# Attention and two MLPs in one kernel: where P is divided, and which operand of P x V is stationary

## The chip, the cores and the metric

The kernel runs on one core of a Trainium2 chip. Time is the device time of one execution in microseconds, and lower is better. The kernel before takes 892.09 us (median of three runs, 891.72 to 892.2). The profile comes from one further execution, of 890.85 us.

## The reference

There are 4 batches, 8 heads, 576 positions and a head size of 64, all in fp32. Heads 0 to 3 see the last 32 positions, heads 4 to 7 see every earlier position of the same residue modulo 32. Two MLPs with squared ReLU follow.

```python
scores = scale * np.matmul(q, k.transpose(0, 1, 3, 2))
mask_local = (rel >= 0) & (rel < stride)                      # heads 0-3
mask_strided = (rel >= 0) & (pos[None, :] % stride == pos[:, None] % stride)   # heads 4-7
scores = np.where(masks[None], scores, -1e9)
attn = np.exp(scores - np.max(scores, axis=-1, keepdims=True))
attn = attn / (np.sum(attn, axis=-1, keepdims=True) + 1e-09)
x = np.matmul(attn, v)                       # -> (2304, 512)
for w_in, w_out in (moe, moe2):              # (512, 2048), (2048, 512)
    x = np.square(np.maximum(x @ w_in, 0)) @ w_out
```

## The kernel before

**The MLPs.** They are what TensorE does most of the time. A layer works on 5 blocks of tokens (512, and one of 256); a block has 16 steps, one for each 128 columns of the hidden width. Products are exact to fp32 by splitting both operands in a high and a low part of type fp32r and adding three products. A step `s` of the main loop issues `mm1(s + 1)`, 12 products of 128x512 into `ps_h`, and then `mm2(s)`, 12 products into `ps_y`. At the end of `mm1`, ScalarE takes the ReLU (`r`, L744) and the square (`gh`, L752), and VectorE the square in fp32 and its low part (`sq`, L753; `gl`, L754). All products have the line L696.

**The attention.** It is cut in 48 fills, numbered 0 to 47, 12 for each batch: a fill is two heads and one piece of the positions. A local fill has 2 groups of 96 queries with 128 keys for each head; a strided one has two groups of 126, two of 108 or one of 108 queries, with as many keys. Of a batch's 12 fills, 6 are local, and of each strided kind there are 2. The MLP of layer 1 needs X of a block before that block starts, so batch 1 runs alone at the start, and batches 2, 3 and 4 run between the products of the blocks 0, 1 and 2 of layer 1.

**The stages of a fill in batches 3 and 4** (fills 24 to 47) are these, and the functions that hold them:
- `split_qk` (L324): q and k are split in high and low parts, two instructions on ScalarE (`qs` L332, `k` L333) and two on VectorE (L334, L337), and the next q and k are loaded into the one buffer for them.
- `scores_first`, `scores_second` (L351): the scores of either head, fp32r.
- `mask_first`, `mask_second` (L379, L381): mask, scale and the negative row maximum, on VectorE.
- `exponent` (L484): one instruction on ScalarE for each head and group.
- `turn_p` (L491): P is transposed by TensorE, one instruction for each head and group; `keep_p` (L499) copies it to SBUF on ScalarE.
- `values` (L507): for each head and group one plain fp32 matmul. Its stationary operand is transposed P (96, 108 or 126 columns), its moving operand is V with a column of ones (65 columns), so that the row sums come with X. It then loads the V of a later fill.
- `divide` (L538 to L541): on VectorE, the sums plus 1e-9, their reciprocal, and X times it.
- `turn_x` (L553): X of both heads is transposed, one instruction for each group.
- `keep_x` (L592) copies X to the MLP's operand as its high part on ScalarE, `rest_x` (L596) subtracts it from X for the low part on VectorE. A fill that lies over a border of blocks does it in parts.

**The order.** A round is one pass through the list `BETWEEN` (L625), in which `(fn, back)` means that the stage `fn` is done for the fill that is `back` fills behind the round's own. So different fills are in different stages at a time. The list has ten places. The rounds of all batches stand one behind the other in `att`, and `att_to` (L650) works them off up to a place. It is called at points in the MLP: `mm1` has a point after each of its first three groups of three products, one stands after `mm1`, three lie in `mm2`, and one follows it, eight to a step. `spans` (L1021) and `point` (L1054) spread the places of a batch evenly over 116 points of its block; in blocks 1 and 2 of layer 1 these are 150 and 120 places. A place whose list is empty only takes room in this spread.

**Queues.** Each engine works its instructions in order. All loads and stores go by the queue of SP, in program order. All PSUM tiles of these fills come in turn from three banks of the pool `ps_a`; `ps_h` has one bank. The tiles `s`, `pt`, `m` and `den` have two buffers each, and V has five.

Of the kernel before, what the change touches and what calls it, by code (L numbers as in the profile page):

```python
# [9 lines left out]
F32 = mybir.dt.float32  # L10
F32R = mybir.dt.float32r
I32 = mybir.dt.int32
AF = mybir.ActivationFunctionType
ALU = mybir.AluOpType
AX = mybir.AxisListType

P = 128
B, H, S, D = 4, 8, 576, 64
STRIDE = 32
NPOS = S // STRIDE  # L20
# [6 lines left out]
BLOCKS = [  # L27
    [(0, TB), (TB, TB), (2 * TB, TB), (3 * TB, TB // 2), (NT - TB, TB)],
    [(0, TB // 2)] + [(n * TB + TB // 2, TB) for n in range(4)],
]  # L30
# [21 lines left out]
FIRST_2 = 2  # L52


SFILLS = [(0, 7, 2), (14, 6, 2), (26, 6, 1)]
LQ, LK = 2 * QB, 2 * QB + STRIDE
# [28 lines left out]
def pack_local(q, k, v):  # L85


    qk = np.zeros((B, 2, 3, P, 2 * LQ + LK), np.float32)
    ov = np.ones((B, 2, 3, P, 2, 2, D + 1), np.float32)
    kp = np.zeros((B, 4, STRIDE + S, D), np.float32)  # L90
    vp = np.zeros((B, 4, STRIDE + S, D), np.float32)
    kp[:, :, STRIDE:] = k[:, :4]
    vp[:, :, STRIDE:] = v[:, :4]
    for u in range(2):
        for f in range(3):
            for h in range(2):
                n, rows = 2 * u + h, slice(h * D, (h + 1) * D)
                qk[:, u, f, rows, h * LQ:(h + 1) * LQ] = q[:, n, f * LQ:(f + 1) * LQ].transpose(0, 2, 1)
                qk[:, u, f, rows, 2 * LQ:] = kp[:, n, f * LQ:f * LQ + LK].transpose(0, 2, 1)
                for g in range(2):  # L100
                    k0 = f * LQ + g * QB
                    ov[:, u, f, :, h, g, :D] = vp[:, n, k0:k0 + P]
    return qk, ov.reshape(B, 2, 3, P, VW)


def pack_strided(q, k, v, fill):

    r0, n, ng = fill
    m = n * NPOS
    w = ng * m  # L110
    qk = np.zeros((B, 2, P, 3 * w), np.float32)
    ov = np.ones((B, 2, P, 2, ng, D + 1), np.float32)

    def rows_of(x):
        x = x[:, 4:].reshape(B, 4, NPOS, STRIDE, D)[:, :, :, r0:r0 + n * ng]
        return x.transpose(0, 1, 3, 2, 4).reshape(B, 4, w, D)

    qq, kk, vv = rows_of(q), rows_of(k), rows_of(v)
    for u in range(2):
        for h in range(2):  # L120
            rows = slice(h * D, (h + 1) * D)
            qk[:, u, rows, h * w:(h + 1) * w] = qq[:, 2 * u + h].transpose(0, 2, 1)
            qk[:, u, rows, 2 * w:] = kk[:, 2 * u + h].transpose(0, 2, 1)
            for g in range(ng):
                ov[:, u, :m, h, g, :D] = vv[:, 2 * u + h, g * m:(g + 1) * m]
    return qk, ov.reshape(B, 2, P, 2 * ng * (D + 1))


def both_halves(qk, w, groups):


    rest = qk.shape[-1] - 2 * w
    kw = rest if groups is None else (groups - 1) * (w // groups) + P
    t = np.zeros(qk.shape[:-1] + (2 * w + 2 * kw,), np.float32)
    for h in range(2):
        rows = slice(h * D, (h + 1) * D)
        for half in (slice(0, D), slice(D, P)):
            t[..., half, h * w:(h + 1) * w] = qk[..., rows, h * w:(h + 1) * w]
            k0 = 2 * w + h * kw
            t[..., half, k0:k0 + rest] = qk[..., rows, 2 * w:]  # L140
    return t


def r32(ap):
    return ap.bitcast(F32)
# [3 lines left out]
def tile_attention_then_two_mlps(  # L149
# [9 lines left out]
    nc = tc.nc  # L159
# [6 lines left out]
    apool = ctx.enter_context(tc.tile_pool(name="att", bufs=2))  # L166
# [128 lines left out]
    fills = []  # L295
# [7 lines left out]
    SPLIT = FIRST_2 * PER_B  # L303
    kin, vin = {}, {}
    n_in, n_vin = [0], [0]

    def src_of(i):
        b, u, kind, f = fills[i]
        arrays, at = (loc, (u, f)) if kind == "l" else (st[f], (u,))
        qk0, qk, v = arrays  # L310
        return (qk0[(b,) + at] if b < FIRST_2 else qk[(b - FIRST_2,) + at]), v[(b,) + at]

    def load_qk():
        i = n_in[0]
        if i >= NFILL:
            return
        n_in[0] += 1
        qk = src_of(i)[0]
        tag = "qk" + str(i % 3 if i < SPLIT else 0)
        kin[i] = fpool.tile([P, QK_COLS[tag]], F32, tag=tag, name="qk", bufs=1)  # L320
        nc.sync.dma_start(out=kin[i][:, :qk.shape[-1]], in_=qk)
# [76 lines left out]
    def load_v():  # L398
        i = n_vin[0]
        if i >= NFILL:  # L400
            return
        n_vin[0] += 1
        _, v = src_of(i)
        vin[i] = vfpool.tile([P, VW], F32, tag="v", name="v", bufs=5)
        nc.sync.dma_start(out=vin[i][:, :v.shape[-1]], in_=v)
# [6 lines left out]
    def x_at(n):  # L412

        return 0 if n == TB else 48

    def x_tiles(j):
        if j not in xh:
            xh[j], xl[j] = (x_tile(t, j % 3) for t in ("xh", "xl"))
        return xh[j], xl[j]

    def geometry(i):

        b, u, kind, f = fills[i]
        if kind == "l":
            return QB, P, 2, QB
        r0, n, ng = SFILLS[f]
        m = n * NPOS
        return m, m, ng, m

    def ps_tile(i, name):  # L430

        n_ps[0] += 1
        if fills[i][0] == 0 and n_ps[0] % 7 < KC:
            return ps_y.tile([P, 512], F32, tag=f"y{n_ps[0] % 7}", name=name)
        return ps_a.tile([P, 512], F32, tag="a", name=name)

    n_ps = [0]
    s_ps, s_sb, mx, pt_ps, pt_sb, o_ps, xn, x_ps = ({} for _ in range(8))
    W = D + 1

# [38 lines left out]
    def exponent(i):  # L479
        nq, nk, ng, _ = geometry(i)  # L480
        s, m = s_sb[i], mx.pop(i)
        for j in range(2 * ng):
            blk = s[:nq, j * nk:(j + 1) * nk]
            nc.scalar.activation(out=blk, in_=blk, func=AF.Exp, scale=-1.0, bias=m[:nq, j:j + 1])  # L484

    def turn_p(i):
        nq, nk, ng, _ = geometry(i)
        s = s_sb.pop(i)
        ps = pt_ps[i] = ps_tile(i, "ps_pt")
        for j in range(2 * ng):  # L490
            nc.tensor.transpose(  # L491
                ps[:nk, j * nq:(j + 1) * nq], s[:nq, j * nk:(j + 1) * nk], ident[:nq, :nq]
            )
# [65 lines left out]
    def x_parts(i):  # L559

        b, u, kind, f = fills[i]
        ps = x_ps[i]
        parts = []
        if kind == "l":
            c = u
            t0, t1 = b * S + f * LQ, b * S + (f + 1) * LQ
            for j, (b0, nb) in enumerate(BLOCKS[0]):
                lo, hi = max(t0, b0), min(t1, b0 + nb)
                if lo < hi:
                    parts.append((j, ps[:, lo - t0:hi - t0], lambda x, a=lo - b0, e=hi - b0, o=x_at(nb): x[:, c, o + a:o + e]))  # L570
        else:
            c = 2 + u
            r0, n, ng = SFILLS[f]
            n *= ng
            src = ps[:, :n * NPOS].rearrange("p (r i) -> p i r", i=NPOS)
            i0 = b * NPOS
            for j, (b0, nb) in enumerate(BLOCKS[0]):
                o, nt = x_at(nb), nb
                b0, nb = b0 // STRIDE, nb // STRIDE
                lo, hi = max(i0, b0), min(i0 + NPOS, b0 + nb)  # L580
                if lo < hi:
                    parts.append((
                        j,
                        src[:, lo - i0:hi - i0],
                        lambda x, a=lo - b0, e=hi - b0, o=o, nt=nt: x[:, c, o:o + nt].rearrange(
                            "p (i r) -> p i r", r=STRIDE)[:, a:e, r0:r0 + n],
                    ))
        return parts

    def keep_x(i):  # L590
        for j, src, place in x_parts(i):
            nc.scalar.activation(out=place(x_tiles(j)[0]), in_=src, func=AF.Copy)  # L592

    def rest_x(i):
        for j, src, place in x_parts(i):
            nc.vector.tensor_tensor(  # L596
                out=place(xl[j]), in0=src, in1=place(r32(xh[j])), op=ALU.subtract
            )
        x_ps.pop(i)
# [23 lines left out]
        [],  # L623
    ]
    BETWEEN = [  # L625
        [(scores_first, 0), (mask_first, 0)],
        [(turn_p, 1)],
        [(keep_p, 1)],
        [(scores_second, 0), (mask_second, 0)],
        [(split_qk, -1)],  # L630
        [(turn_x, 2)],
        [(keep_x, 2)],
        [(rest_x, 2), (exponent, 0)],
        [(values, 1), (divide, 1)],
        [],
    ]
    att = []
# [375 lines left out]
    for k, s in first.items():  # L1013

        s, lag, each = (first[NB], 2, 1) if k == NB + 1 else (s - 12, 3, 2)
# [7 lines left out]
    with tc.manual_schedule():  # L1023
# [3 lines left out]
        ps = ps_h.tile([P, TB], F32, tag="h", name="ps_w")[:, :P]  # L1027
# [18 lines left out]
        for s in range(len(steps)):  # L1046
            k, f = steps[s]
            layer, j = blocks[k]
# [68 lines left out]
```

## Time and profile before

| | before |
|---|---|
| median of three runs | 892.09 us |
| the profiled execution | 890.85 us, span 889.1 us |
| TensorE busy | 870.4 us (98%) |
| VectorE busy | 630.7 us (71%) |
| ScalarE busy | 491.1 us (55%) |
| values, P x V (L507), all batches | 352 instructions |
| transposes of X (L553), all batches | 88 instructions |

A busy time is the union of an engine's instructions. TensorE's instructions are pipelined: a row of one lasts longer than the engine is taken by it, and neighbours overlap. In the timeline, equal neighbours are merged in a row with their count; its first number is the start from the beginning of the span, its second the duration from the first start to the last end. Plain fp32 matmuls count twice, since each is two instructions; transposes and fp32r products count once.

### The profile page before, as it was taken

Reading aid. Unit: us, or ns where it says so; the run is one execution under the profiler, and the core shown is the slowest. Engines: PE = TensorE matmul, PEld = TensorE weight load, DVE = VectorE, ACT = ScalarE, POOL = GpSimd, SP = SyncE. Lnnn points to the kernel's source line nnn. Section 1 sums busy time; section 2 is a strip of 40 time slices with the busy share of each in tenths; the row PEclk is TensorE's granted clock in tenths of the full one; section 3 lists DMA queues with packets and bytes.
Section 4 is the critical chain, followed back from the end, with each engine's and each line's share of the span. In section 5 each row is a group of like instructions: output and inputs, shape, how many; then the busy total and the mean of one; then the engine's idle time right before and its main releaser. Section 6 shows DMA issues by size and latency. Waiting matters only on the chain.

```text
span 889.1 us, 14160 instructions
## 1 busy us (share of the span) xinstructions
PE 870.4 (98%) x5290; PEld 762.1 (86%) x5290; DVE 630.7 (71%) x1521; ACT 491.1 (55%) x987; POOL 0.2 (0%) x4
## 2 busy tenths in 40 slices
PE   9699999999999999999999999999999999999997
PEld 8578878888888888899888898899999999999996
DVE  6999973477765666322299996677787787778676
ACT  6787863455555554232377885545545555555443
POOL 0000000000000000000000000000000000000000
PEclk9799999999999999999999999999999999999999
DMA  8966610222223210010566530100020010001001
GB/s 264 322 216 222 197 42 19 83 79 71 71 77 98 80 52 24 2 48 1 175 209 208 166 131 13 48 13 13 1 73 18 8 49 24 24 1 49 1 1 48
DMA packets 45940, 72.02 MB, mean 81 GB/s; under 512 B 3504, under 2 KB 32304, under 8 KB 45872
## 3 DMA queue, kind: packets, MB, share of 16 engines
q1 hardware_dynamic: 45872, 71.12, 24.5%
q8 instruction: 42, 0.69, 0.3%
q14 instruction: 26, 0.21, 0.1%
HBM read 61.67 MB, written 9.44 MB: 80 GB/s over the span
## 4 chain that ended last, share of the span: by engine, by line
PE 87%; DVE 9%; ACT 2%; issue 1%; ACTq 0%; DVEq 0%
PE ps_h L696 41%; PE ps_y L696 21%; PE ps_y L917 17%; PE ps_o L507 3%; DVE raw L223 2%; PE ps_pt L491 2%; DVE w L268 1%; DVE val L234 1%; PE ps_s L351 1%; PE ps_s L448 1%; DVE raw L220 1%; DVE gl L754 1%; PE ps_x L553 1%; DVE s L468 1%; DVE xl L596 1%
## 5 line engine op out<-in xcount | busy, mean ns | idle before, releaser
L696 PE MATMUL ps_h<-xh,w 128*128 128x512 f32 (+1 forms) x1344 | 401.0, 364 | 0.0
L696 PEld LDWEIGHTS ps_h<-xh,w 128*128 128x128 f32 x1344 | 245.0, 188 | 39.0
L696 PE MATMUL ps_h<-xl,w 128*128 128x512 f32 (+1 forms) x640 | 235.9, 369 | 0.0
L696 PE MATMUL ps_y<-gh,w 128*128 128x512 f32 (+1 forms) x640 | 157.2, 375 | 0.0
L696 PEld LDWEIGHTS ps_h<-xl,w 128*128 128x128 f32 x640 | 120.9, 189 | 14.8 <-DVE xl L596 0.2
L696 PEld LDWEIGHTS ps_y<-gh,w 128*128 128x128 f32 x640 | 107.7, 188 | 16.4 <-ACT gh L750 0.2
L744 ACT ACTIVATE r<-ps_h 128x512 f32<-128x512 f32 x80 | 47.7, 596 | 120.5 <-PE ps_h L696 83.8
L753 DVE TENSOR_TENSOR sq<-r 128x512 f32<-128x512 f32 x50 | 34.6, 692 | 101.6 <-ACT r L744 101.4
L861 DVE TENSOR_TENSOR xl<-wf,xh 128x768 fp32r<-128x768 f32 (+1 forms) x80 | 80.0, 1010 | 15.6 <-ACT xh L860 15.3
L696 PE MATMUL ps_y<-gl,w 128*128 128x512 f32 (+1 forms) x324 | 85.4, 371 | 0.0
L738 DVE TENSOR_TENSOR sq<-sq 128x512 f32<-128x512 f32 x64 | 44.1, 689 | 53.1 <-ACT sq L737 53.1
L860 ACT ACTIVATE xh<-wf 128x768 fp32r<-128x768 f32 (+1 forms) x80 | 68.9, 880 | 22.0 <-PE ps_y L917 22.0
L737 ACT ACTIVATE sq<-ps_h 128x512 f32<-128x512 f32 x64 | 37.8, 591 | 71.8 <-PE ps_h L696 64.9
L917 PE MATMUL ps_y<-xh,gbl 128*128 128x256 f32 x256 | 70.9, 277 | 0.3 <-DVE gbl L861 0.3
L917 PE MATMUL ps_y<-xh,gbh 128*128 128x256 f32 x256 | 71.1, 278 | 0.0
L917 PE MATMUL ps_y<-xl,gbh 128*128 128x256 f32 x256 | 70.9, 277 | 0.0
L754 DVE TENSOR_TENSOR gl<-sq,gh 128x512 fp32r<-128x512 f32 x80 | 55.2, 691 | 20.6 <-ACT gh L750 14.6
L696 PEld LDWEIGHTS ps_y<-gl,w 128*128 128x128 f32 x324 | 55.3, 188 | 8.8
L484 ACT ACTIVATE s<-s,m 96x128 f32<-96x128 f32 (+2 forms) x176 | 55.6, 388 | 5.2 <-DVE m L468 4.8
L917 PE MATMUL ps_y<-xl,gah 128*128 128x256 f32 x192 | 53.3, 278 | 0.2 <-DVE xl L861 0.2
L917 PE MATMUL ps_y<-xh,gal 128*128 128x256 f32 x192 | 53.2, 277 | 0.2 <-DVE gal L882 0.2
L917 PE MATMUL ps_y<-xh,gah 128*128 128x256 f32 x192 | 53.3, 278 | 0.0
(77 smaller groups left out, 1347.0 us busy)
## 6 DMA issues: line engine op xcount, KB each, us to landing
raw<-moe_w_in_d SPq DMA_DIRECT2D x32, 512.0 KB, 4.7
raw<-moe_w_out_d SPq DMA_DIRECT2D x32, 512.0 KB, 4.0
qk<-loc_qk_d SPq DMA_DIRECT2D x12, 416.0 KB, 3.2
out_d<-o SPq DMA_DIRECT2D x18, 256.0 KB, 2.3
y_dram<-o SPq DMA_DIRECT2D x16, 256.0 KB, 2.1
y_in<-y_dram SPq DMA_DIRECT2D x16, 256.0 KB, 3.0
qk<-loc_qk_d SPq DMA_DIRECT2D x12, 304.0 KB, 4.0
v<-loc_v_d SPq DMA_DIRECT2D x24, 130.0 KB, 2.5
```

What stands on the lines that cost most here:

```text
L223: nc.vector.scalar_tensor_tensor(out=lower, in0=upper, scalar=-(2 ** 31), in1=lower, op0=ALU.bitwise_and, op1=ALU.bitwise_or)
L484: nc.scalar.activation(out=blk, in_=blk, func=AF.Exp, scale=-1.0, bias=m[:nq, j:j + 1])
L507: nc.tensor.matmul(ps[:nq, j * W:(j + 1) * W], lhsT=pt[:nk, j * nq:(j + 1) * nq], rhs=t[:nk, j * W:(j + 1) * W], start=True, stop=True,)
L696: nc.tensor.matmul(y[:, c:c + w], lhsT=lhsT, rhs=rhs[:, c:c + w], start=start and c == 0, stop=stop and c + w == n,)
L737: nc.scalar.activation(out=t, in_=ps, func=AF.Relu, scale=W_BACK)
L738: nc.vector.tensor_tensor(out=t, in0=t, in1=t, op=ALU.mult)
L744: nc.scalar.activation(out=r, in_=ps, func=AF.Relu, scale=W_BACK)
L753: nc.vector.tensor_tensor(out=sq, in0=r, in1=r, op=ALU.mult)
L754: nc.vector.tensor_tensor(out=lo, in0=sq, in1=r32(h), op=ALU.subtract)
L860: nc.scalar.activation(out=hi, in_=src, func=AF.Copy)
L861: nc.vector.tensor_tensor(out=lo, in0=src, in1=r32(hi), op=ALU.subtract)
L917: nc.tensor.matmul(y[:, t * HALF:(t + 1) * HALF], lhsT=a[:, i, rows], rhs=w[:, cols], start=first and t == 0 and m == 0, stop=end and t == ...
```

## The change

It touches the fills of batches 3 and 4 alone. The exponents also give the row sums (`exponent_and_sums`), `divide_p` divides P by them in place on VectorE, ahead of the transposing. `values_of_both` then does one matmul for each group: its stationary operand is V of both heads side by side (128 columns, packed so on the host, without the column of ones), its moving operand transposed P of both heads. The result is X already transposed, with head 0 in the partitions 0 to 63 of the first half of its columns and head 1 in the partitions 64 to 127 of the second half; the other quarters aren't read. `turn_x` and `divide` drop out. `keep_x` and `rest_x` take X by halves of 64 partitions (`x_parts_of_both`), and where a local fill lies over a border of blocks, also by group. The places of the stages in a round are new; the values of a fill come one round after its scores, as before, and its X in that same round rather than in the one behind.

```diff
+def heads_together(v, groups):
+    v = v.reshape(v.shape[:-1] + (2, groups, D + 1))[..., :D]
+    return np.ascontiguousarray(v.swapaxes(-3, -2)).reshape(v.shape[:-3] + (groups * P,))
...
+    def exponent_and_sums(i):
+        nq, nk, ng, _ = geometry(i)
+        s, m = s_sb[i], mx.pop(i)
+        d = dens[i] = apool.tile([P, 4], F32, tag="den", name="den")
+        for j in range(2 * ng):
+            blk = s[:nq, j * nk:(j + 1) * nk]
+            nc.scalar.activation(
+                out=blk, in_=blk, func=AF.Exp, scale=-1.0, bias=m[:nq, j:j + 1],
+                accum_out=d[:nq, j:j + 1],
+            )
+
+    def divide_p(i):
+        nq, nk, ng, _ = geometry(i)
+        d = dens.pop(i)[:nq, :2 * ng]
+        nc.vector.tensor_scalar_add(out=d, in0=d, scalar1=1e-9)
+        nc.vector.reciprocal(out=d, in_=d)
+        s = s_sb[i][:nq, :2 * ng * nk].rearrange("q (j k) -> q j k", j=2 * ng)
+        nc.vector.tensor_tensor(
+            out=s, in0=s, in1=d.unsqueeze(2).to_broadcast([nq, 2 * ng, nk]), op=ALU.mult
+        )
+
+    def values_of_both(i):
+        nq, nk, ng, _ = geometry(i)
+        pt = pt_sb.pop(i)[:nk, :2 * ng * nq].rearrange("k (h g q) -> k h g q", h=2, g=ng)
+        v = vin.pop(i)
+        ps = x_ps[i] = ps_tile(i, "ps_x")
+        for g in range(ng):
+            nc.tensor.matmul(
+                ps[:, 2 * g * nq:2 * (g + 1) * nq],
+                lhsT=v[:nk, g * P:(g + 1) * P],
+                rhs=pt[:, :, g],
+                start=True,
+                stop=True,
+            )
+        load_v()
+
+    def x_parts_of_both(i):
+        b, u, kind, f = fills[i]
+        nq, nk, ng, _ = geometry(i)
+        parts = []
+        for h in range(2):
+            rows = slice(h * D, (h + 1) * D)
+            ps = x_ps[i][rows, :2 * ng * nq].rearrange("p (g h q) -> p h g q", g=ng, h=2)[:, h]
...
     def keep_x(i):
-        for j, src, place in x_parts(i):
+        for j, src, place in (x_parts if i < SPLIT else x_parts_of_both)(i):
             nc.scalar.activation(out=place(x_tiles(j)[0]), in_=src, func=AF.Copy)
 
     def rest_x(i):
-        for j, src, place in x_parts(i):
+        for j, src, place in (x_parts if i < SPLIT else x_parts_of_both)(i):
...
     BETWEEN = [
-        [(scores_first, 0), (mask_first, 0)],
+        [(divide_p, 1), (scores_first, 0), (mask_first, 0)],
+        [],
+        [(scores_second, 0), (mask_second, 0)],
         [(turn_p, 1)],
         [(keep_p, 1)],
-        [(scores_second, 0), (mask_second, 0)],
         [(split_qk, -1)],
-        [(turn_x, 2)],
-        [(keep_x, 2)],
-        [(rest_x, 2), (exponent, 0)],
-        [(values, 1), (divide, 1)],
+        [(values_of_both, 1)],
+        [(keep_x, 1), (exponent_and_sums, 0)],
+        [(rest_x, 1)],
         [],
     ]
...
-        arrays[name + "_v"] = vals
+        arrays[name + "_v0"] = vals[:FIRST_2]
+        arrays[name + "_v"] = heads_together(vals[FIRST_2:], ng)
```

## Rows read from the trace of the kernel before

**Rows 1.** The page, the chain that ended last, by engine.

```profile
PE 87%; DVE 9%; ACT 2%; issue 1%; ACTq 0%; DVEq 0%
```

**Rows 2.** Busy time by stretch: us, then each engine, granted clock, DMA share, GB/s.

```profile
169.00:270.00 101.00, 100.72 (x551) 82.82 (x550) 70.03 (x242) 54.83 (x139) 0.00 (x0) 1.00 0.25 78
270.00:372.00 102.00, 102.00 (x550) 85.02 (x549) 59.02 (x194) 47.98 (x119) 0.00 (x0) 1.00 0.16 51
```

**Rows 3.** TensorE's timeline, a local round: start, us, line, operands, count.

```profile
199.93 0.84 PE L696 MATMUL ps_y<-gh,w 128*128 128x512 f32 x3
200.61 0.33 PE L553 MATMUL ps_x<-cst,xn 96*128 96x96 f32 x2
200.72 1.40 PE L696 MATMUL ps_y<-gh,w 128*128 128x512 f32 x5
201.96 0.40 PE L696 MATMUL ps_y<-gl,w 128*128 128x512 f32 x1
202.20 0.81 PE L507 MATMUL ps_o<-v,pt 128*96 128x65 f32 x8
202.82 0.94 PE L696 MATMUL ps_y<-gl,w 128*128 128x512 f32 x3
```

**Rows 4.** TensorE's timeline, the values of a strided fill.

```profile
222.46 1.62 PE L696 MATMUL ps_y<-gh,w 128*128 128x512 f32 x6
223.92 0.99 PE L507 MATMUL ps_o<-v,pt 126*126 126x65 f32 x8
224.72 0.71 PE L696 MATMUL ps_y<-gh,w 128*128 128x512 f32 x2
225.27 1.08 PE L696 MATMUL ps_y<-gl,w 128*128 128x512 f32 x4
```

**Rows 5.** TensorE's timeline, plain fp32 scores of a fill of an earlier batch.

```profile
81.06 0.94 PE L696 MATMUL ps_y<-gl,w 128*128 128x512 f32 x3
81.84 1.04 PE L448 MATMUL ps_s<-qk 128*96 128x128 f32 x8
82.63 0.48 PE L696 MATMUL ps_h<-xh,w 128*128 128x512 f32 x1
```

**Rows 6.** TensorE's timeline, scores that waited for the split.

```profile
175.19 0.39 PE L696 MATMUL ps_h<-xh,w 128*128 128x512 f32 x1
175.71 0.45 PE L351 MATMUL ps_s<-k,qs 128*96 128x256 f32 x2
176.00 0.49 PE L491 MATMUL ps_pt<-cst,s 96*128 96x96 f32 x4
```

**Rows 7.** ScalarE's timeline in a local round.

```profile
197.77 0.49 ACT L499 ACTIVATE pt<-ps_pt 128x384 f32<-128x384 f32 x1 [1.34 <-PE ps_pt L491]
200.18 0.60 ACT L744 ACTIVATE r<-ps_h 128x512 f32<-128x512 f32 x1 [1.92 <-DVE m L381]
200.80 0.63 ACT L752 ACTIVATE gh<-r 128x512 fp32r<-128x512 f32 x1
...
202.22 0.31 ACT L592 ACTIVATE xh<-ps_x 128x192 fp32r<-128x192 f32 x1
202.43 1.27 ACT L484 ACTIVATE s<-s,m 96x128 f32<-96x128 f32 x4
```

**Rows 8.** VectorE's timeline in the same round.

```profile
198.10 0.08 DVE L381 DVE_READ_ACCUMULATOR2_ANT m<- 96x1 f32 x1
...
200.80 0.69 DVE L753 TENSOR_TENSOR sq<-r 128x512 f32<-128x512 f32 x1 [0.41 <-ACT r L744]
...
203.46 0.35 DVE L596 TENSOR_TENSOR xl<-ps_x,xh 128x192 fp32r<-128x192 f32 x1
```

**Rows 9.** ScalarE by shape from 165 to 375 us: the exponent, the shortest row.

```profile
L484 ACT ACTIVATE s<-s,m 96x128 f32<-96x128 f32 x48 | 15.3, 390 | 0.1
...
L592 ACT ACTIVATE xh<-ps_x 128x12 fp32r<-128x12 f32 x2 | 0.3, 168 | 2.9 <-PE ps_x L553 2.9
```

**Rows 10.** The page's DMA issues: count, KB each, us to landing.

```profile
qk<-loc_qk_d SPq DMA_DIRECT2D x12, 416.0 KB, 3.2
...
v<-loc_v_d SPq DMA_DIRECT2D x24, 130.0 KB, 2.5
```

More of the change, by code (lines that the diff above doesn't have):

```diff
@@ L309, in src_of @@
         arrays, at = (loc, (u, f)) if kind == "l" else (st[f], (u,))
-        qk0, qk, v = arrays
-        return (qk0[(b,) + at] if b < FIRST_2 else qk[(b - FIRST_2,) + at]), v[(b,) + at]
+        qk0, qk, v0, v = arrays
+        if b < FIRST_2:
+            return qk0[(b,) + at], v0[(b,) + at]
+        return qk[(b - FIRST_2,) + at], v[(b - FIRST_2,) + at]
     def load_qk():
@@ L435, in ps_tile @@
         return ps_a.tile([P, 512], F32, tag="a", name=name)
-    n_ps = [0]
+    n_ps, dens = [0], {}
     s_ps, s_sb, mx, pt_ps, pt_sb, o_ps, xn, x_ps = ({} for _ in range(8))
@@ new lines, in x_parts_of_both @@
+    def x_parts_of_both(i):
[5 more added lines that the diff above has]
+            ps = x_ps[i][rows, :2 * ng * nq].rearrange("p (g h q) -> p h g q", g=ng, h=2)[:, h]
+            if kind == "l":
+                for j, (b0, nb) in enumerate(BLOCKS[0]):
+                    o = x_at(nb)
+                    t0 = b * S + f * LQ
+                    if b0 <= t0 and t0 + LQ <= b0 + nb:
+                        a = o + t0 - b0
+                        parts.append((j, ps, lambda x, r=rows, a=a: x[r, u, a:a + LQ].rearrange(
+                            "p (g q) -> p g q", g=ng)))
+                        continue
+                    for g in range(ng):
+                        t1 = t0 + g * nq
+                        lo, hi = max(t1, b0), min(t1 + nq, b0 + nb)
+                        if lo < hi:
+                            parts.append((
+                                j, ps[:, g, lo - t1:hi - t1],
+                                lambda x, r=rows, a=o + lo - b0, e=o + hi - b0: x[r, u, a:e],
+                            ))
+                continue
+            r0, n, _ = SFILLS[f]
+            src = ps.rearrange("p g (r i) -> p g i r", i=NPOS)
+            i0 = b * NPOS
+            for j, (b0, nb) in enumerate(BLOCKS[0]):
+                o, nt = x_at(nb), nb
+                b0, nb = b0 // STRIDE, nb // STRIDE
+                lo, hi = max(i0, b0), min(i0 + NPOS, b0 + nb)
+                if lo < hi:
+                    parts.append((
+                        j, src[:, :, lo - i0:hi - i0],
+                        lambda x, r=rows, a=lo - b0, e=hi - b0, o=o, nt=nt: x[r, 2 + u, o:o + nt].rearrange(
+                            "p (i r) -> p i r", r=STRIDE)[:, a:e, r0:r0 + n * ng].rearrange(
+                            "p i (g r) -> p g i r", g=ng),
+                    ))
+        return parts
@@ L1090 @@
     arrays = {"consts": const_table()}
-    for name, w, groups, (qk, vals) in [("loc", LQ, None, pack_local(q, k, v))] + [
-        (f"st{i}", fill[1] * fill[2] * NPOS, fill[2], pack_strided(q, k, v, fill))
+    for name, w, groups, ng, (qk, vals) in [("loc", LQ, None, 2, pack_local(q, k, v))] + [
+        (f"st{i}", fill[1] * fill[2] * NPOS, fill[2], fill[2], pack_strided(q, k, v, fill))
         for i, fill in enumerate(SFILLS)
@@ L1108 @@
             aps["consts"],
-            [aps["loc" + n] for n in ("_qk0", "_qk", "_v")],
-            [[aps[f"st{i}" + n] for n in ("_qk0", "_qk", "_v")] for i in range(len(SFILLS))],
+            [aps["loc" + n] for n in ("_qk0", "_qk", "_v0", "_v")],
+            [[aps[f"st{i}" + n] for n in ("_qk0", "_qk", "_v0", "_v")] for i in range(len(SFILLS))],
             [aps["moe_w_in"].bitcast(I32), aps["moe2_w_in"].bitcast(I32)],
```

## The prediction

> **What bounds the kernel now.** I read the chain of waits first: 87% of the span's last chain is TensorE [rows 1]. Then the busy time by stretch: batches 3 and 4 of the attention are worked off between about 169 and 372 us, and TensorE is busy in 100.72 of 101 us and in 102 of 102 us there, at a granted clock of 1.00 (2.4 GHz), while VectorE is at 69% and 58% and ScalarE at 54% and 47% [rows 2]. So an instruction that leaves TensorE in these stretches shortens the span by the time it takes in its stream, and work on VectorE or ScalarE costs nothing unless TensorE comes to wait for it. TensorE's durations overlap (the row of one lasts longer than its place in the stream), so I price by ends: from the end of the row before to the end of the row behind, less the products of the MLP in between. Such a product takes 0.23 us (four in 1.08 us, the last lasting about 0.39) [rows 4].
>
> **What leaves TensorE.** A local fill's two transposes of X: from 200.77 to 202.12 is 1.35 us with five products (1.15), so 0.20 us. Its four value matmuls, each two instructions because the operands are plain fp32: from 202.36 to 203.76 is 1.40 us with three products, so 0.71 us [rows 3]. For the strided fill of 126 queries the values take, from 224.08 to 225.43, 1.35 less two products: 0.89 us [rows 4]. For 108 queries I take 0.79, between the two by the width of the stationary operand, and for the fill of one group half, 0.40; transposes 0.21, 0.21 and 0.11. There are 24 fills: 12 x 0.91 + 4 x 1.10 + 4 x 1.00 + 4 x 0.51 = 21.4 us go.
>
> **What comes in.** One matmul for each group, V of both heads stationary (128 columns), P of both heads moving: 192 columns local, 252 and 216 strided, again plain fp32 and so two instructions. The nearest rows are the plain fp32 scores of batch 2: eight instructions with 128 moving columns against 96 stationary ones, from 82.00 to 83.11 less one product, 0.88 us, so 0.110 us for one or 0.86 ns per column [rows 5]. The value matmuls with the same 96 stationary columns and 65 moving ones take 0.71 / 8 = 0.089, so at 128 columns the moving side sets the pace, and it does so all the more at 192. One instruction: 192 x 0.86 = 0.165 us, 252: 0.217, 216: 0.186. Sum: 12 x 4 x 0.165 + 4 x 4 x 0.217 + 4 x 4 x 0.186 + 4 x 2 x 0.186 = 15.8 us. Net on TensorE: -5.6 us.
>
> Bounds of that price: the load of a stationary operand shows where the moving side is short, 0.89 / 8 = 0.11 us at 126 columns [rows 4]; wholly unhidden it adds 88 x 0.11 = 9.7 us. Nothing in the rows points below 0.86 ns per column, so the other end is the same 15.8.
>
> A rule of the Trainium skill speaks against the change: "TensorE: Matmul & The Clock Gate", Part 3, The mechanism, says that a weight load overlaps running matmuls only where its row group differs, and these matmuls all use the full height. By it each new instruction would pay its load besides its stream, and the sum would end 9.7 us higher, at 897 instead of 887. The rows disagree: 0.110 us at 128 moving columns leaves no room for a load of 96 columns beside a stream of 128 [rows 5], so I keep a small chance for it.
>
> **The stalls that go.** TensorE now waits a little for the key split of the next fill: from 175.58 to 176.16 is 0.58 us for two score matmuls that take 0.23 unwaited (0.12 each), so 0.35 us [rows 6]; a second such place stands at 211.29, in all 0.7 us. In the new order the split stands directly behind the keeping of P and the next scores five places later. Written out with the same pacing, in the second block of layer 1 it is issued ahead of the ReLU of the step, where before it stood behind ReLU and square (r and gh, 1.26 us on ScalarE [rows 7]). I count these 0.7 us as gone; if they stay, that is the cost.
>
> **What is added beside TensorE.** The division moves ahead of the transposing, over 512 elements in SBUF: like the square of 128x512, 0.69 us [rows 8], with the two tiny steps about 1.0 us; the old one had half the elements. X is kept and subtracted by halves of 64 partitions, so each part costs again: 0.31 on ScalarE and 0.35 on VectorE for 192 columns [rows 7, 8]. I count half the partitions at the full price; two in a row on ScalarE take 0.53, since neighbours there overlap by 0.1 (four exponents of 0.39 take 1.27). The exponent now also sums: the trace has no ScalarE sum. Its price x for one lies between nothing (it rides along) and 0.39, a second exponent (four take 1.27 us, one 0.39); the shortest ScalarE row is 0.17 us, and the accumulator read of VectorE, the same kind of step, is 0.08 us [rows 7 to 9]. I take 0.08. Per fill some 0.6 us more on VectorE and 0.5 on ScalarE: 14 and 13 us over 203 us with 74 and 100 us idle [rows 2]. The idle time hides them, except where the chain gets short.
>
> The same goes for the queues. V's loads have 128 KB where they had 130, and are issued two places earlier; SP works in order, and the loads of q and k, issued one place later in the round, land in 3.2 us [rows 10] against a round of 7 us until they are read. PSUM: four tiles a fill instead of five go through the three banks, and each bank is free at least two places before its next use. I put all this at nothing; its cover is one round.
>
> **The new waits.** Before, X of a fill came two rounds behind its scores; now a fill closes one round behind, so the chain values, keep X, exponents of the next fill, divide, transpose P, keep P, values is tight. I wrote out both orders by the pacing (141 places over 116 points in block 1, 120 over 116 in block 2; a point every three products, 0.69 us; r and gh ahead of the fourth point of a step). In block 1, r and gh fall between the exponents and the next keeping of P in nearly all rounds, and divide ends over 2 us ahead of its transposes. In block 2 the phase drifts, and three rounds are tight.
> - Fills 40 and 45: the transposes stand at the third point, r and gh come next on ScalarE, then keep P. From the end of the first product group: 1.26 + 0.49 = 1.75 us [rows 7] plus handovers of about 0.1; the values are due six products (1.38 us) later. Stall 0.5 us each.
> - Fill 39: the values of 38 stand at the third point. From there 0.66 + 0.69 to the end of the group, 1.26 for r and gh, 0.53 for X, 1.27 + 4x for the exponents, 1.0 for the division: 5.4 + 4x. The transposes are due after 0.66, 18 products (4.14) and two pairs of scores (0.47): 5.3. Stall, with a handover, 0.25 + 4x = 0.6 us.
> Together 1.6 us. A wait of VectorE for the exponents holds the next fill's mask and the gl product of the MLP behind it; gl isn't read for some 6 us, so TensorE doesn't feel it. Bounds: nothing, if ScalarE runs further ahead than I think; with x = 0.39, 1.2 us more at fill 39 and about 1 and 0.8 at fills 44 and 45's transposes: 4.8.
>
> **Sum.** -5.6 - 0.7 + 1.6 = -4.7 us. The profiled execution took 890.85 us (span 889.1), so its like would take 886.1; it lies 1.24 under the median of the runs shown, so the median comes to 892.09 - 4.7 = 887.4. With stalls at either end: 885.8 to 890.6. Behind 372 us nothing changes but the start: TensorE is the bound there too.
>
> **Rivals.**
> - No new wait: ScalarE and VectorE keep ahead as before; -6.3, 885.8 us. For it: the few waits before; against it: a round's slack is halved.
> - Stalls in most rounds of block 2, some 0.25 us in 10 more: -4.7 + 2.5, 889.9. For it: r and gh are in the way of the chain in most of its rounds.
> - It doesn't do what it says: stalls give back what TensorE saves, 4 us or more over the 1.6; within 1.8 us of before, about 891.
> - Slower, by the loop closing: values 0.66, X 0.53, exponents 1.27 + 4x, division 1.0, transposes 0.49 [rows 6], keep P 0.49, six handovers 0.3, and r and gh 1.26 if they fall inside: 6.0 + 4x against a round of some 7.1 us in block 1 (24 products and the fill's own share). It decides from x = 0.28, and passes the gain at x = 0.41 (12 rounds of 0.54 = 6.5 us). At x = 0.6: 12 x 1.3 = 15.6 us, 892.1 - 6.3 + 15.6 = 901. Against it: that is beyond a whole second exponent, and the order keeps r and gh out of the loop there.
> - Slower, by loads that aren't hidden: 887.4 + 9.7 = 897. This is what the rule above would give. Against it: rows 5.
>
> **How the numbers follow.** My forecast 0.52, no new wait 0.17, stalls in block 2 0.11, given back 0.12, loop 0.05, loads 0.03. The first three are faster by over 0.2% (1.8 us, about what a measurement of this kernel can tell from no change): 0.80; within 0.2%: 0.12; slower: 0.08. The range: 885.0 leaves room for a somewhat cheaper column under the case without waits, 890.3 takes in the stalls of block 2; outside lie the last three cases.
>
> **What would show it.** The value matmuls grouped by shape: 176 instructions before become 88, 0.165 us apart in local fills; if 0.27, the loads aren't hidden. No transposes of X behind 169 us. TensorE's idle time before the transposes of P and before the values, about 1.6 us in all, in the rounds named; if above 5, the chain is the bound. A ScalarE row for the sum, of about 0.08 us: from 0.3 on the loop counts. The waits for the key split gone. The stretch of batches 3 and 4 some 4.7 us shorter, and everything behind it as long as before. I am wrong if the span from there to the end changes by over 1 us, or if TensorE's stream in these stretches doesn't shrink by 5 to 6 us.

## The result, and the profile after

The changed kernel takes 904.18 us (median of four runs, 902.59 to 905.34) against 891.9 us before: a ratio of 1.0137, 95% interval 1.0118 to 1.0155. It is slower by 1.4%, where I had forecast 0.5% faster. The profiled execution took 902.59 us (span 900.7), 11.7 more than the one of before.

Busy time by stretch, the changed kernel, columns as in [rows 2]:

```profile
169.00:270.00 101.00, 91.17 (x450) 74.59 (x450) 71.75 (x234) 57.71 (x182) 0.00 (x0) 1.00 0.21 68
270.00:372.00 102.00, 98.23 (x476) 80.36 (x475) 70.27 (x233) 60.22 (x192) 0.00 (x0) 1.00 0.19 61
```

TensorE, busy without a break before, now idles 9.8 and 3.8 us. Neither VectorE nor ScalarE is full, so something waits in turn. What TensorE waited for, over the stretch of batches 3 and 4 (us in total, times, longest):

```profile
PE ps_pt L580 <- DVE s L514: 12.7, 11, 2.1
...
PE ps_s L359 <- DVE k L345: 0.9, 1, 0.9
PE ps_x L524 <- ACT pt L588: 0.9, 2, 0.5
```

The transposes of P (L580) wait for the division (L514), eleven times: in fills 28 to 34, 38, 39, 43 and 47. Here is one such place, fill 29. First ScalarE's timeline, the end of the exponents and the next step's ReLU and square:

```profile
213.65 0.39 ACT L503 ACTIVATE s<-s,m 96x128 f32<-96x128 f32 x1
213.94 0.19 ACT L503 ACTIVATION_READ_ACCUMULATOR s<-s,m 96x1 f32 x1
214.04 0.39 ACT L503 ACTIVATE s<-s,m 96x128 f32<-96x128 f32 x1
214.33 0.19 ACT L503 ACTIVATION_READ_ACCUMULATOR s<-s,m 96x1 f32 x1
215.01 0.60 ACT L833 ACTIVATE r<-ps_h 128x512 f32<-128x512 f32 x1 [0.49 <-PE ps_h L785]
215.64 0.63 ACT L841 ACTIVATE gh<-r 128x512 fp32r<-128x512 f32 x1
```

VectorE's timeline at the same time, whole, without a row left out:

```profile
212.87 0.72 DVE L685 TENSOR_TENSOR xl<-ps_x,xh 64x192 fp32r<-64x192 f32 x2 [0.16 <-ACT xh L681]
215.64 0.69 DVE L842 TENSOR_TENSOR sq<-r 128x512 f32<-128x512 f32 x1 [2.04 <-ACT r L833]
216.44 0.69 DVE L843 TENSOR_TENSOR gl<-sq,gh 128x512 fp32r<-128x512 f32 x1
217.05 0.16 DVE L511 TENSOR_SCALAR den<-den 96x4 f32<-96x4 f32 x1
217.24 0.17 DVE L512 RECIPROCAL den<-den 96x4 f32<-96x4 f32 x1
217.45 0.69 DVE L514 TENSOR_TENSOR s<-s,den 96x512 f32<-96x512 f32 x1
```

And TensorE's:

```profile
215.91 0.87 PE L785 MATMUL ps_y<-gh,w 128*128 128x512 f32 x3
218.28 0.52 PE L580 MATMUL ps_pt<-cst,s 96*128 96x96 f32 x4 [1.50 <-DVE s L514]
```

The exponents and sums are done at 214.52. VectorE is idle from 213.59, and yet the division begins at 217.05. In between VectorE sits 2.04 us waiting for the ReLU, since `sq` (L842) and `gl` (L843) stand ahead of the division in its queue, and the ReLU can't start before the products of `mm1` end, at 214.92. The division then ends at 218.14, and TensorE has waited 1.50 us. VectorE's idle time here isn't spare room: it is the wait itself.

What TensorE does has become shorter as forecast. The values of a local fill, in TensorE's timeline of the changed kernel, answer to [rows 3]:

```profile
210.64 0.86 PE L785 MATMUL ps_y<-gl,w 128*128 128x512 f32 x3
211.33 0.81 PE L524 MATMUL ps_x<-pt,v 128*128 128x192 f32 x4
211.84 0.53 PE L785 MATMUL ps_h<-xh,w 128*128 128x512 f32 x1
```

From 211.50 to 212.37 is 0.87 us with one product, so 0.64 us for four instructions, 0.16 each, where values and transposes of X took 0.91 us before.

### The profile page after: what moved, and what is told of

It is laid out like the page before. It is cut to its first block, busy times and chain, and to the rows that moved or that the text cites. A ratio compares the mean times of both kernels' runs of the same rounds, so it can differ in the third digit from the quotient of the medians.

```text
span 900.7 us, 14043 instructions
## 1 busy us (share of the span) xinstructions
PE 865.1 (96%) x5158; PEld 755.9 (84%) x5158; DVE 647.0 (72%) x1563; ACT 510.5 (57%) x1117; POOL 0.2 (0%) x4
## 4 chain that ended last, share of the span: by engine, by line
PE 79%; DVE 13%; ACT 5%; issue 2%; DMA 1%; SPq 0%; DVEq 0%; ACTq 0%
PE ps_h L785 39%; PE ps_y L785 18%; PE ps_y L1006 17%; DVE raw L229 2%; PE ps_x L524 2%; DVE w L274 2%; DVE val L240 2%; DVE gl L843 1%; ACT s L503 1%; PE ps_pt L580 1%; ACT r L833 1%; DVE raw L226 1%; DVE s L476 1%; DVE sq L842 1%; DVE s L514 1%
## 5 line engine op out<-in xcount | busy, mean ns | idle before, releaser
L842 DVE TENSOR_TENSOR sq<-r 128x512 f32<-128x512 f32 x50 | 34.6, 691 | 101.4 <-ACT r L833 101.4
L843 DVE TENSOR_TENSOR gl<-sq,gh 128x512 fp32r<-128x512 f32 x80 | 55.2, 690 | 21.3 <-ACT gh L839 15.0
L235 ACT ACTIVATE raw<-raw 128x512 f32<-128x512 f32 x64 | 43.3, 676 | 12.9 <-DVE raw L229 12.9
```

The lines of the kernel that those rows point to most:

```text
L235: nc.scalar.activation(out=upper, in_=upper, func=AF.Copy, scale=2.0 ** (W_EXP // 8 - 112))
L842: nc.vector.tensor_tensor(out=sq, in0=r, in1=r, op=ALU.mult)
L843: nc.vector.tensor_tensor(out=lo, in0=sq, in1=r32(h), op=ALU.subtract)
```

## The experiments

Theory A: the division stands behind `sq` and `gl` in VectorE's queue, and it is this order that costs. Rival B: the exponents with their sums end too late. Rival C: the division is too long for the distance to the transposes. E1 to E4 ran beside the kernel before at 892.37 us, E5 to E8 at 891.56, E9 and E10 at 891.52, so versions of different sets are compared by their ratios to it.

**E1, the division two places earlier.**

```diff
-        [(divide_p, 1), (scores_first, 0), (mask_first, 0)],
+        [(scores_first, 0), (mask_first, 0)],
...
-        [(rest_x, 1)],
+        [(rest_x, 1), (divide_p, 0)],
```

> The changed kernel with one edit: the division of P stands two places earlier in the round, behind the subtraction of X (place 8, same round) instead of at the start of the next. In block 1 and most of block 2 it is then issued on VectorE ahead of the step's sq and gl. Theory A (the division waits in VectorE's queue behind sq and gl, which wait for the end of the first product group, and the transposes of P wait for it): the waits of the transposes for the division before fills 28 to 38, 43 and 47 go, about 13 us, leaving the one at fill 39 and those at values and scores: 889 to 892 us. Rival B (the exponents with sums end too late, wherever the division stands): the division starts no earlier, 900 us or more. Rival C (the division's own 1.1 us is too long for the distance): still a wait in most rounds, 897 us or more.

Measured: 889.06 us, ratio 0.9966 (0.9953 to 0.9979). One line of the order moved takes some 15 us off the changed kernel and makes it faster than before. VectorE's timeline at fill 29:

```profile
213.02 0.72 DVE L685 TENSOR_TENSOR xl<-ps_x,xh 64x192 fp32r<-64x192 f32 x2
214.25 0.17 DVE L511 TENSOR_SCALAR den<-den 96x4 f32<-96x4 f32 x1 [0.52 <-ACT s L503]
214.45 0.17 DVE L512 RECIPROCAL den<-den 96x4 f32<-96x4 f32 x1
214.66 0.69 DVE L514 TENSOR_TENSOR s<-s,den 96x512 f32<-96x512 f32 x1
215.32 0.69 DVE L842 TENSOR_TENSOR sq<-r 128x512 f32<-128x512 f32 x1
```

The ReLU and the transposes, from the timelines of ScalarE and TensorE:

```profile
214.69 0.60 ACT L833 ACTIVATE r<-ps_h 128x512 f32<-128x512 f32 x1 [0.47 <-PE ps_h L785]
216.31 0.50 PE L580 MATMUL ps_pt<-cst,s 96*128 96x96 f32 x4
```

The division starts when the exponents end, and `sq` comes behind it, no later than it would have: the ReLU is done only at about 215.3. The transposes at 216.31 don't wait. One wait for the division is left, 0.9 us at fill 39, where the exponents themselves stand behind the ReLU.

**E2, no sums.** The output is then not the reference's, since P is divided by ones.

```diff
             nc.scalar.activation(
                 out=blk, in_=blk, func=AF.Exp, scale=-1.0, bias=m[:nq, j:j + 1],
-                accum_out=d[:nq, j:j + 1],
             )
...
-        nc.vector.tensor_scalar_add(out=d, in0=d, scalar1=1e-9)
+        nc.vector.memset(d, 1.0)
```

> The changed kernel without the sums of the exponents: P is divided by ones, so the output isn't the reference's; order and division as in the changed kernel. Theory A: the division is held by gl and not by the exponents, so little changes, 0.37 us in those rounds where the ReLU stands behind the exponents on ScalarE: 901 to 903.5 us. Rival B (sums make the exponents late): 10 us or more go, 894 us or less.

Measured: 898.73 us, ratio 1.0076 (1.0061 to 1.0091). This lies between the theories' numbers, nearer to A and in the range of neither. The waits for the division are still there, 9.5 us in 10 places against 12.7 in 11, so most of them don't come from the sums. But the sums cost more than I gave them. TensorE's timeline, the transposes of fills 28 to 31, of the changed kernel:

```profile
209.55 0.52 PE L580 MATMUL ps_pt<-cst,s 96*128 96x96 f32 x4 [1.51 <-DVE s L514]
218.28 0.52 PE L580 MATMUL ps_pt<-cst,s 96*128 96x96 f32 x4 [1.50 <-DVE s L514]
227.22 0.62 PE L580 MATMUL ps_pt<-cst,s 126*126 126x126 f32 x4 [1.74 <-DVE s L514]
236.53 0.37 PE L580 MATMUL ps_pt<-cst,s 108*108 108x108 f32 x2 [1.38 <-DVE s L514]
```

and without the sums:

```profile
208.89 0.52 PE L579 MATMUL ps_pt<-cst,s 96*128 96x96 f32 x4 [1.44 <-DVE s L513]
217.55 0.52 PE L579 MATMUL ps_pt<-cst,s 96*128 96x96 f32 x4 [1.43 <-DVE s L513]
226.22 0.62 PE L579 MATMUL ps_pt<-cst,s 126*126 126x126 f32 x4 [1.46 <-DVE s L513]
235.09 0.55 PE L579 MATMUL ps_pt<-cst,s 108*108 108x108 f32 x4 [0.94 <-DVE s L513]
```

A round of the changed kernel lasts 8.7 to 9.3 us, against 7.4 before (from the values at 202.20 in [rows 3] to the next, at 209.59). In the first two rows the waits differ by 0.07 us, and that isn't the sums: the memset that stands in for the addition (L511) takes 0.06 us on VectorE instead of 0.16. In the third and fourth rows they differ by 0.28 and 0.44. There, in the changed kernel, the late transposes have made the values, X and the exponents so late that the ReLU finds ScalarE busy with the exponents:

```profile
223.74 0.18 ACT L503 ACTIVATION_READ_ACCUMULATOR s<-s,m 126x1 f32 x1
223.95 0.60 ACT L833 ACTIVATE r<-ps_h 128x512 f32<-128x512 f32 x1
```

The chain has closed here: exponents, ReLU, `sq`, `gl`, division, transposes, keep P, values, X, next exponents. Where it is closed, each 0.1 us of the exponents counts, so the sums' 0.37 us a fill do too. The chain that ended last shows it, in the round of fill 30. In the changed kernel it comes to the ReLU over the exponents, without the sums over TensorE's products:

```profile
222.28 1.41 ACT s L503 x7
...
223.95 0.61 ACT r L833
```

```profile
220.84 2.10 PE ps_h L784 x9
...
223.01 0.61 ACT r L832
```

Between 169 and 270 us the exponents are 5.9% of that chain in the changed kernel and 1.1% without the sums. So two things add up. The order on VectorE makes waits by itself, with no closed chain: 1.43 to 1.46 us in the first three rows without the sums. The sums close the chain in some rounds and lengthen the waits there: in fills 30, 31, 33, 34, 38, 39 and 43 the wait is 0.3 to 0.7 us longer with them, in fills 28, 29, 32 and 47 0.07 at most.

**E3, no division.** Sums and division are left out, so P stays undivided and the output isn't the reference's.

```diff
-        [(divide_p, 1), (scores_first, 0), (mask_first, 0)],
+        [(scores_first, 0), (mask_first, 0)],
```

> The changed kernel without sums and without the division (P stays undivided, so the output isn't the reference's). Theory A: the transposes wait for the exponents alone, all their waits go (about 15 us), and what is left shows what TensorE's stream saves: 887 to 890 us. If the time lay in the values with V stationary or anywhere else on TensorE, it would stay above 897 us.

Measured: 886.78 us, ratio 0.9944 (0.9927 to 0.996): 5.6 us less than before, and just under A's range. The loss doesn't lie in the values with V stationary; TensorE's saving is real and was covered by the waits.

**E4, a loose round.** All operations of the change, in an order near that of before. The new list, whole:

```diff
     BETWEEN = [
+        [(rest_x, 2), (scores_first, 0), (mask_first, 0)],
+        [(turn_p, 1)],
+        [(keep_p, 1)],
+        [(scores_second, 0), (mask_second, 0)],
+        [(split_qk, -1)],
+        [(exponent_and_sums, 0), (divide_p, 0)],
+        [],
+        [],
+        [(values_of_both, 1)],
+        [(keep_x, 1)],
     ]
```

> The changed kernel's operations in an order near that of before: exponents and division together in place 5, transposes of P in place 1 of the next round, values in place 8, X kept in place 9 and subtracted at the start of the round behind. The division is issued ahead of sq and gl, and transposes and values have 6 and 6 places. Theory A: nearly no waits on TensorE, so its saving of 5.6 us shows whole: 885 to 888 us, faster than before. Rival B or C: the transposes still wait in block 1, above 893 us.

Measured: 886.5 us, ratio 0.9938 (0.9923 to 0.9952). With division and sums it is as fast as E3 without them. One wait for the division is left, at fill 37, 1.37 us.

**E5, `sq` and `gl` behind the division.** Here no stage of a fill moves; only the two VectorE instructions of the MLP are issued two points later, in the blocks 1 and 2 of layer 1.

```diff
-            nc.vector.tensor_tensor(out=sq, in0=r, in1=r, op=ALU.mult)
-        nc.vector.tensor_tensor(out=lo, in0=sq, in1=r32(h), op=ALU.subtract)
+            if NF <= s < 3 * NF:
+                behind.append(lambda: nc.vector.tensor_tensor(out=sq, in0=r, in1=r, op=ALU.mult))
...
+        def low():
+            nc.vector.tensor_tensor(out=lo, in0=sq, in1=r32(h), op=ALU.subtract)
+
+        if behind:
+            behind.append(low)
...
+                while behind and n_pt[0] in (6, 7, 8):
+                    behind.pop(0)()
```

> The changed kernel; no stage of a fill is moved. In the blocks 1 and 2 of layer 1 VectorE's sq and gl are issued two points later, behind the division, instead of at the end of the first product group. Theory A (it is the order in VectorE's queue, not the place of the division in the round): the division starts when the exponents end, the waits of the transposes for it in fills 28 to 38, 43 and 47 go: 888 to 892 us. Rival (sums or division too long for the round): the waits stay, 900 us or more.

Measured: 889.36 us, ratio 0.9973 (0.9963 to 0.9982). VectorE's timeline at fill 29:

```profile
212.84 0.17 DVE L511 TENSOR_SCALAR den<-den 96x4 f32<-96x4 f32 x1 [0.57 <-ACT s L503]
...
213.25 0.69 DVE L514 TENSOR_TENSOR s<-s,den 96x512 f32<-96x512 f32 x1
...
215.72 0.68 DVE L844 TENSOR_TENSOR sq<-r 128x512 f32<-128x512 f32 x1
216.50 0.69 DVE L849 TENSOR_TENSOR gl<-sq,gh 128x512 fp32r<-128x512 f32 x1
```

This separates the order in the queue from the place in the round: the division has its place of the changed kernel, the sums and its length are unchanged, and the time is gone. B and C fall as causes of the loss; the sums only add to it, as E2 shows. The waits for the division left are 1.9 us in three places.

**E6, the changed kernel again**, on the chip of E5.

> The changed kernel itself, on the same chip as the others of this set: 902 to 905 us.

Measured: 902.04 us, ratio 1.0117 (1.01 to 1.0134).

**E7, the split behind the division.** From the loose round, meant to take its last wait away.

```diff
-        [(split_qk, -1)],
         [(exponent_and_sums, 0), (divide_p, 0)],
+        [(split_qk, -1)],
```

> The loose round, with exponents and division one place earlier and the split of the next q and k one place later. The one wait left in the loose round (1.4 us before the transposes at the start of block 2, where the exponents are issued right behind the ReLU) should go, since they now stand ahead of it: 1 to 1.5 us less than the loose round, 884.5 to 886 us. If the split then comes too late for the next scores, that shows as waits of the scores for the key split, and the time stays at 886 to 888.

Measured: 903.67 us, ratio 1.0128 (1.0109 to 1.0146), by the ratios 17 us more than the loose round, and 14.4 us between the two profiled executions. My forecast missed: the wait named as the risk came, but with it I had put the time at 886 to 888 us. The waits, then the timelines of VectorE and TensorE at one of them:

```profile
DVE den L511 <- ACT s L503: 18.6, 23, 3.1
ACT s L503 <- DVE m L389: 15.1, 22, 2.3
PEld ps_s L359 <- issue: 14.5, 12, 2.8
...
PE ps_s L359 <- DVE k L345: 12.0, 12, 2.4
```

```profile
207.74 0.17 DVE L511 TENSOR_SCALAR den<-den 96x4 f32<-96x4 f32 x1 [0.74 <-ACT s L503]
207.94 0.17 DVE L512 RECIPROCAL den<-den 96x4 f32<-96x4 f32 x1
208.15 0.69 DVE L514 TENSOR_TENSOR s<-s,den 96x512 f32<-96x512 f32 x1
208.87 0.56 DVE L342 TENSOR_TENSOR qs<-qk,qs 64x384 fp32r<-64x384 f32 x1
209.45 0.62 DVE L345 TENSOR_TENSOR k<-qk,k 128x448 fp32r<-128x448 f32 x1
...
210.22 0.45 PE L359 MATMUL ps_s<-k,qs 128*96 128x256 f32 x2 [0.60 <-DVE k L345]
```

It is the same fault the other way round. The split needs nothing from this fill, but on VectorE it now stands behind the division, that waits for the exponents, and these for the second mask; the next scores wait for the split, 0.60 us at 210.22.

**E8, the loose round without sums.** The edit is that of E2, made to E4; P is again divided by ones.

> The loose round without the sums of the exponents (P is divided by ones, so the output isn't the reference's). If the sums cost only in a closed chain (theory A), this is within 0.6 us of the loose round, 885.9 to 887.1. If the sums, 96 instructions on ScalarE with 0.09 us each in the changed kernel, cost in any order, it is 3 us or more below.

Measured: 885.97 us, ratio 0.994 (0.9925 to 0.9955); the loose round has 0.9938. The same sums (88 of them, not the 96 I had written) that cost some 4 us in the changed kernel cost nothing here that the intervals, 1.3 us to either side, can show.

**E9, transposes one place later**, and **E10, the loose round again**, together.

```diff
         [(rest_x, 2), (scores_first, 0), (mask_first, 0)],
+        [],
         [(turn_p, 1)],
-        [(keep_p, 1)],
-        [(scores_second, 0), (mask_second, 0)],
+        [(keep_p, 1), (scores_second, 0), (mask_second, 0)],
```

> The loose round with the transposes of P and the keeping of P one place later, everything else as it was. The division and the split keep their order on VectorE, so no new wait for the split (unlike the version with the split behind the division). The one wait of the loose round, 1.4 us before the transposes of fill 37 at the start of block 2, shrinks by a point of the MLP (0.7 us) or goes: 0.5 to 1.5 us less than the loose round on the same chip. If the time doesn't move, the wait has only changed its place.

> The loose round again, beside the version with later transposes: 885.5 to 887 us, 0.993 to 0.995 of before.

Measured: E9 885.63 us (885.29 to 886.08), ratio 0.9933 (0.992 to 0.9945); E10 886.57 us (886.23 to 887.26), ratio 0.9943 (0.9929 to 0.9956). The runs of the two don't overlap. In E9 the last wait has 0.53 us left of 1.37, and TensorE's stretches are full again:

```profile
169.00:270.00 101.00, 100.88 (x500) 84.05 (x499) 79.19 (x260) 62.68 (x202) 0.00 (x0) 1.00 0.23 73
270.00:372.00 102.00, 101.47 (x505) 84.72 (x504) 68.46 (x224) 57.57 (x188) 0.00 (x0) 1.00 0.18 56
```

E9 is the fastest version, 5.9 us under the kernel before. VectorE is busier in it (78% of the first stretch) than in the changed kernel (71%): the load wasn't the trouble.

## Why the prediction was wrong

**Right: TensorE's stream.** 0.16 us an instruction against 0.165, 88 of them. Priced by ends in the trace, what left and what came in differ by 5.6 us, as forecast. E3 and E4 bear it out with 5.6 and 5.9 us less than before; these are net of waits, with old ones gone and some 1.5 us of others left, so that they agree to the tenth is partly luck.

**Right: no load beside the stream.** A stationary operand of 128 columns at 0.16 us for 192 moving ones leaves no room for its load. The rule that speaks against the change ("TensorE: Matmul & The Clock Gate" of the Trainium skill, Part 3, The mechanism: a load overlaps only matmuls of another row group) doesn't hold in this trace.

**Right in size: the sum.** An exponent follows the last after 0.39 us (213.65 to 214.04) instead of 0.29 ([rows 7]: four in 1.27), so a sum costs 0.1 us; I took 0.08.

**Right, but not all: the tight rounds of block 2.** I named 0.5 us each for the values of fills 40 and 45, and 0.6 for the transposes of fill 39; the trace has 0.41, 0.50 and 0.89 us of idle time there. I did not name the transposes of fills 38, 43 and 47 (0.34, 0.73 and 1.02 us). The old waits for the key split went as forecast, but the scores of fill 46 now wait 0.91 us for it. The upper bound for the new waits, 4.8 us, comes to 4.6 by its own terms; nothing hangs on that.

**Wrong: the step on block 1.** I wrote that r and gh fall between the exponents and the next keeping of P, "and divide ends over 2 us ahead of its transposes". The first half is true, and is the trouble. In fills 28 to 36, and again in 38, 43 and 47, the ReLU of the step is issued before the division; on ScalarE the exponents are ahead of it, but on VectorE `sq` and `gl` are ahead of the division, and they wait for the ReLU. All of these but 35 and 36 make TensorE wait; the eleventh wait is that of fill 39. At fill 29 TensorE stood 1.50 us waiting for the division that should have been over 2 us ahead. The prediction has r and gh in the way on ScalarE alone; of VectorE's queue it asks only who stands behind the waiting division, not behind whom it stands. So the term for new waits, 1.6 us, should have been about 17: by ends, as in the pricing of the prediction, the eleven waits for the division take 14.8 us, and those at values and scores 2.6. With -5.6 for the stream and -1.2 for the old waits of the scores, that gives 10.6 us. Between the ends of the same two products, at 165.5 and 389.2 us in the kernel before, the changed one takes 10.5 us more. The rest of the 11.7 between the two profiles lies ahead of 165 us, where no work has changed; there the other profiled runs are 0 to 2.5 us longer than the kernel before, and why isn't explained.

**Half right: the loop.** I had it as the rival that ends slower, at 901, but made it hang on the price of a sum, from 0.28 us on, and gave it 0.05. With a sum of 0.1 us it closed all the same in some rounds of the changed kernel: its length was counted without `sq` and `gl`, 1.4 us, and it was held open by an order that I had read wrongly. But it is the smaller part of the loss. Without the sums (E2) it is open in most of these rounds, and the kernel is still 0.8% slower than before.

## What to carry to other kernels

Before a stage is given a new place, write out the order on every engine that it issues to, one round after the other, and ask of each instruction what stands ahead of it and what that waits for; an engine at 70% busy can still be late. In an in-order queue, an instruction that waits for a distant event belongs behind those that are ready sooner and needed sooner. A gain on the bounding engine is worth looking for again after such a loss: here one line of the order won back the loss and over half of the gain (E1), and another order all of it (E4, E9).

## What the runs showed that I had not expected

A small cost beside the bound can be worth nothing or half its size, depending on the order: the 88 sums of 0.1 us, 8.8 us of ScalarE in all, cost some 4 us where they closed the chain (E2 against E6, the shorter memset included) and nothing measurable where it was open (E8 against E4). And two neighbouring places exchanged (E4 against E7) make 17 us, more than the whole change.
